# The first nine tiles of a fused attention and channel-mix kernel in another order, with more warm-up and filler products

## The chip, the cores and the metric

The kernel runs on one core of one Trainium2 chip. The time is the device time of one execution in microseconds; lower is better. The kernel before takes 1877.62 us (median of 3 runs, 1877.34 to 1879.11).

## The reference

Queries attend to keys that are pooled 4x4 and projected (the values are the same as the keys). The result goes through a channel mix with a shift by one token: two mixes of a token with the one before it, a squared ReLU layer of width 1024, and a sigmoid gate.

```python
# B, C = 4, 128; N = 12288 tokens, 768 pooled keys, d_ff = 1024
kv_pool = kv.reshape(B, H // 4, 4, W // 4, 4, C).mean(axis=(2, 4))
k = v = kv_pool.reshape(B, -1, C) @ w_sr
s = (q @ k.transpose(0, 2, 1)) / np.sqrt(C)
a = np.exp(s - s.max(-1, keepdims=True)); a /= a.sum(-1, keepdims=True) + 1e-09
x = a @ v
x_prev = np.concatenate([zeros, x[:, :-1, :]], axis=1)
xk = mu_k * x + (1.0 - mu_k) * x_prev
xr = mu_r * x + (1.0 - mu_r) * x_prev
kk = np.maximum(xk @ w_k, 0.0)
out = 1.0 / (1.0 + np.exp(-(xr @ w_r))) * (kk * kk @ w_v)
```

## The kernel before, in words

The tokens are cut into 97 tiles: two of 256 tokens at the start, then tiles of 512. All is kept with the channel on the partitions. Numbers are split into a high and a low half (`qh`, `ql`; `xkh`, `xkl`; `kh`, `kl`; `wkh`, `wkl`), and products are summed over the halves. A tile runs through named steps, each on one engine; `.4` behind a name is the tile:

- `qf` loads the queries (SP), `qh` casts them (ACT), `ql` is the rest (POOL).
- `S0` to `S3`: six score products for each 128 tokens (PE) into a `big` buffer of PSUM, of which there are three. `nm` takes the maximum (DVE), `ex` the exponential `pe` and its sum (ACT), `rc` the reciprocal (DVE: a tensor_scalar and a reciprocal), `f1` and `f2` make the high and low half of the weights `pp` (ACT and DVE), and `tt` transposes them by DMA (SP) into `pT`.
- `AV0` to `AV5`: 18 products `px` (PE). `xek`, `xer` (ACT), `xk`, `xr` (DVE) mix with the token before, for which POOL copies one column (`xck`, `xcr`); `xkh`, `xrh` cast (DVE), `xkl`, `xrl` subtract (POOL).
- `z`: three products for the gate, then `th`, `E` (ACT), `T1`, `E1`, `g` (DVE; the profile shows them as `th` and `E`).
- `ha`, `hb`: the products `ph` of the first layer, in four groups, into `big`. `r` is the ReLU `rr` (ACT), `k2` its square `kk` (DVE for groups 0, 1 and 3, ACT for 2), `kh` the cast (ACT for 0, 1, 3; DVE for 2), `kl` the rest (POOL for 0 to 2, DVE for 3).
- `va`, `vb`: the products `pv` of the second layer, into the one `v` buffer; `o` multiplies by the gate (DVE), `so` stores (SP). The next tile's `pv` can start when `o` has read the buffer.

Ahead of the tiles stand one-time steps: the pooled keys of the first batch (`L_a`, `L_b` load, `ad`, `bd` add on DVE, `pa`, `pb` project on PE, `ks`, `kh0_`, `kb0_`, `kl0_` and the like store the halves `ks`, `ksh`, `ksb`, `ksl`), the weights (`L_`, `we_`, `wl_`, `wi_`, `wt_`, `wc_`, `wx_`, `wy_`, `wg_`, `wh_`, `wd_` of `wk`, `wv`, `wr`), and scales (`am`, `ex`, `dg`, `xm`, `xt`, `sv`, `uz`, `cz`, `cv`). `warm` is a row of products of constants `pw` at the start. The keys of the next batch are loaded and summed during the tiles (`L_kv`, `br`, which writes `acc`).

The order is a table of numbers. Every step is put on one heap with its number; `give` takes the least and emits the step's instructions, and each engine keeps that order:

```python
def add(self, when, name, fn, of):
    heapq.heappush(self.heap, (when, next(self.count), fn, name, of))

def give(self):
    while self.heap:
        heapq.heappop(self.heap)[2]()
```

`ONCE` has the numbers of the one-time steps, `EARLY` those of the first nine tiles (one table each), `WHEN` those of all tiles in the middle (plus 19.3 times the tile), `LATE` those of the last ones. The numbers only order the steps; semaphores between engines make them wait for what they need. Nearly every instruction shows line 41 in the profile, that of the helper which emits it, so groups are told by tiles. `BUSY` may name groups of filler products, which write a `pw` tile in the `v` buffer:

```python
for i, n in enumerate(BUSY):
    @once(f"busy{i}")
    def _(n=n):
        if not busy:
            busy.append(take("v", name="pw", shape=[P, 2 * P]))
        for _ in range(n):
            pe.matmul(busy[0], lhsT=ones_b, rhs=ones.bitcast(BF16), start=True, stop=True)
```

Of the kernel before, what the change touches and what calls it, by code (L numbers as in the profile page):

```python
# [80 lines left out]
def tile_kernel(ctx, tc, qT, kv0, kvw, wmu, w_k, w_v, w_r, outT):  # L81
# [85 lines left out]
    busy = []  # L167
    for i, n in enumerate(BUSY):
        @once(f"busy{i}")
# [661 lines left out]
    for i, (b, t0, W) in enumerate(spans):  # L831
# [24 lines left out]
WARM = 48  # L856
BUSY = []
# [56 lines left out]
        "xer": 99.976, "xek": 101.1, "xk": 102.223, "xkh": 107.841, "ha1": 108.964, "xkl": 110.088,  # L914
# [8 lines left out]
    },  # L923
    {
# [14 lines left out]
    },  # L939
    {  # L940
# [7 lines left out]
        "xek": 169.203, "xk": 171.66, "xr": 172.151, "xkh": 175.59, "xkl": 176.082, "xrh": 181.144,  # L948
# [8 lines left out]
    },  # L957
    {
# [7 lines left out]
        "xek": 182.079, "xer": 182.287, "xr": 182.391, "xk": 182.495, "xkh": 182.599,  # L966
# [225 lines left out]
```

## Time and profile before

| | |
|---|---|
| median of 3 runs | 1877.62 us |
| the profiled execution | 1877.43 us, of which the span from first to last instruction 1875.7 us |
| PE, DVE, ACT, POOL busy, share of the span | 98%, 94%, 91%, 62% |
| granted TensorE clock | 1.000 |
| DMA | 232.16 MB, mean 124 GB/s |

The profile is of one execution. Times are in us from its first instruction. A group's row gives its count, its busy time, the mean length of one in ns, and the idle time ahead of it; a row in order of time gives start and length, and in brackets how long the engine had stood idle and what ended that. PE is the matrix engine TensorE, DVE VectorE, ACT ScalarE, POOL GpSimd, SP the engine that issues the DMAs. A DVE row counts as busy from its start to its end, whatever it does between.

### The profile page before, as it was taken

How to read it: one execution, taken by the hardware profiler on the slowest of the kernel's cores; microseconds unless marked ns; L12 is line 12 of the kernel's file. 1: busy time of each engine (PE TensorE's matmuls, PEld its weight loads, DVE VectorE, ACT ScalarE, POOL GpSimd, SP SyncE). 2: the span in 40 equal slices, each digit the busy share in tenths (PEclk: the TensorE clock that was granted, in tenths of full speed). 3: DMA queues.
4: the chain of work that ended last, by engine and by line, in shares of the span. 5: the costliest groups of instructions: out<-in, count | busy, mean ns of one | idle time of the engine just before them, and what ended most of it. 6: DMA issues, size and time to landing. Idle time of an engine off the chain costs nothing.

```text
span 1875.7 us, 27101 instructions
## 1 busy us (share of the span) xinstructions
PE 1843.9 (98%) x8978; PEld 923.3 (49%) x9124; DVE 1766.3 (94%) x2559; ACT 1703.8 (91%) x2448; POOL 1165.0 (62%) x800
## 2 busy tenths in 40 slices
PE   8999999999999999999999999999999999999999
PEld 4544445444444444444545454544444444444444
DVE  7999999999999999999998999999999898989998
ACT  6988899999999999999999999999999999999987
POOL 2554657575666666666656575756665656666555
PEclk9999999999999999999999999999999999999999
DMA  7756665555656666555656565655564655555552
GB/s 248 151 119 138 137 129 130 103 117 115 118 113 140 136 141 140 125 112 107 127 107 141 130 145 133 143 117 113 102 128 102 121 104 116 110 112 108 104 110 57
DMA packets 644236, 232.16 MB, mean 124 GB/s; under 512 B 612352, under 2 KB 613120, under 8 KB 644096
## 3 DMA queue, kind: packets, MB, share of 16 engines
q1 hardware_dynamic: 644096, 230.43, 58.5%
q8 instruction: 72, 1.18, 0.3%
q14 instruction: 68, 0.56, 0.1%
HBM read 52.63 MB, written 25.17 MB: 41 GB/s over the span
## 4 chain that ended last, share of the span: by engine, by line
PE 85%; DVE 9%; issue 1%; ACT 1%; POOL 0%; DVEq 0%; ACTq 0%
PE ph L41 24%; PE pv L41 22%; PE S L41 18%; PE px L41 17%; PE pz L41 3%; DVE pp L41 2%; DVE nm L41 2%; DVE kk L41 1%; DVE rc L41 0%; DVE kl L41 0%; DVE E L41 0%; DVE xk L41 0%; DVE xr L41 0%; DVE ph L41 0%; DVE o L41 0%
## 5 line engine op out<-in xcount | busy, mean ns | idle before, releaser
L41 POOL TENSOR_TENSOR kl<-kk,kh 128x1024 bf16<-128x1024 f32 (+1 forms) x291 | 683.3, 2349 | 59.4 <-DVE kk L41 17.6
L41 POOL TENSOR_TENSOR xrl<-xr,xrh 128x512 f16<-128x512 f32 (+1 forms) x97 | 113.7, 1172 | 514.1 <-DVE xrh L41 508.2
L41 DVE TENSOR_REDUCE nm<-S 128x1 f32<-128x768 f32 x384 | 364.2, 949 | 70.2 <-PE S L41 69.2
L41 DVE SCALAR_TENSOR_TENSOR pp<-pe,rc,pp 128x768 f16<-128x768 f32 x384 | 419.3, 1110 | 7.8 <-ACT pp L41 7.8
L41 PE MATMUL px<-pT,vT 128*128 128x512 f16 (+1 forms) x1746 | 420.6, 377 | 0.6 <-ACT E L41 0.5
L41 ACT ACTIVATE rr<-ph 128x1024 f32<-128x1024 f32 (+1 forms) x388 | 390.7, 1008 | 32.9 <-PE ph L41 31.1
L41 ACT ACTIVATE pe<-S,nm 128x768 f32<-128x768 f32 x384 | 344.2, 896 | 60.2 <-DVE nm L41 58.7
L41 ACT ACTIVATE pp<-pe,rc 128x768 f16<-128x768 f32 x384 | 339.8, 930 | 44.0 <-ACT pe L41 36.8
L41 ACT ACTIVATE kh<-rr 128x1024 f16<-128x1024 f32 (+1 forms) x291 | 304.5, 1047 | 0.9
L41 PE MATMUL ph<-xkh,wkl 128*128 128x512 f16 (+1 forms) x776 | 292.1, 377 | 4.4 <-DVE kl L41 1.7
L41 PE MATMUL pv<-kh,wvl 128*128 128x512 f16 (+1 forms) x776 | 292.0, 377 | 2.8 <-DVE o L41 2.8
L41 PE MATMUL ph<-xkh,wkh 128*128 128x512 f16 (+1 forms) x776 | 292.1, 377 | 0.0
L41 PE MATMUL pv<-kh,wvh 128*128 128x512 f16 (+1 forms) x776 | 292.0, 377 | 0.0
L41 PEld LDWEIGHTS <-vT 128*128 128x128 f16 x1746 | 170.6, 98 | 201.4 <-issue 1.3
L41 PE MATMUL S<-ksb,ql 128*128 128x256 bf16 (+1 forms) x762 | 249.9, 328 | 7.9 <-ACT pe L41 2.5
L41 PEld LDWEIGHTS <-wkh 128*128 128x128 f16 x1552 | 151.6, 98 | 172.3 <-issue 3.4
L41 DVE TENSOR_TENSOR kk<-ph,rr 128x1024 f32<-128x1024 f32 (+1 forms) x194 | 233.8, 1207 | 2.3 <-ACT rr L41 2.1
L41 PEld LDWEIGHTS <-wvh 128*128 128x128 f16 x1552 | 151.7, 98 | 170.5 <-issue 1.4
L41 PE MATMUL ph<-xkl,wkh 128*128 128x512 f16 (+1 forms) x776 | 229.2, 377 | 2.2
L41 PE MATMUL S<-ksl,qh 128*128 128x256 bf16 (+1 forms) x723 | 214.9, 323 | 0.4
L41 PE MATMUL pv<-kl,wvh 128*128 128x512 bf16 (+1 forms) x681 | 206.6, 377 | 0.4
L41 POOL TENSOR_TENSOR xkl<-xk,xkh 128x512 f16<-128x512 f32 (+1 forms) x97 | 145.8, 1503 | 76.2 <-DVE xkh L41 74.6
(126 smaller groups left out, 2484.5 us busy)
## 6 DMA issues: line engine op xcount, KB each, us to landing
qf<-qT SPq DMA_DIRECT2D x95, 256.0 KB, 3.4
outT<-o SPq DMA_DIRECT2D x95, 256.0 KB, 3.0
kvt<-kvw SPq DMA_DIRECT2D x36, 512.0 KB, 4.1
pT<-pp SPq DMA_TRANSPOSE x384, 3.8
kva<-kv SPq DMA_DIRECT2D x8, 512.0 KB, 9.0
kvb<-kv SPq DMA_DIRECT2D x4, 512.0 KB, 5.5
raw<-moe_w_v SPq DMA_DIRECT2D x2, 512.0 KB, 5.4
raw<-moe_w_k SPq DMA_DIRECT2D x2, 512.0 KB, 7.8
```

The costliest lines, as they stand in the source:

```text
L41: return self.tc.keep_in_program_order(op(*args, **kwargs))
```

## The change

The tables `ONCE` and `EARLY` get other numbers, `WARM` goes from 48 to 62, and `BUSY` gets two groups, of 10 and 14 products. `WHEN`, `LATE` and all functions stay. Each engine gets the same instructions as before and PE 38 more. The two filler groups stand among the score steps of the third tile: ten behind `S1` of the second tile, ahead of `S0.2`, and fourteen between `S3.2` and `S2.2`. From a place in tile 8 to 12 on (which one, depends on the engine) every engine's list is the old one; on PE it is the step `vb1` of tile 8.

```diff
-WARM = 48
-BUSY = []
+WARM = 62
+BUSY = [10, 14]
...
 ONCE = {
-    "L_wv1": -98.877, "we_wv1": -97.753, "warm": -96.63, "L_wv0": -95.506, "we_wv0": -94.383,
...
+    "warm": -98.95, "L_wv0": -97.9, "mix": -96.85, "we_wv0": -95.8, "wl_wv0": -94.75,
...
+    "wz_wr0": 40.713, "wh_wr0": 41.763, "cz": 42.813, "sv": 43.863, "busy0": 47.713,
+    "wd_wr0": 56.464, "busy1": 64.515, "cv": 91.117, "uz": 92.167, "wd_wv0": 99.518,
 }
```

Three places, as the engines get them. The first is on ACT, where the first batch's keys are stored (`pk` is their sum in PSUM, the 128x512 part and the 128x256 part; `qh` of the first two tiles). Before:

```order
L41 CAST qh_345<-qf_343 128x256
L41 CAST qh_354<-qf_352 128x256
L41 ACTIVATE ksb_91<-pk_186 128x512
L41 ACTIVATE ks_88<-pk_320 128x256
L41 ACTIVATE ksh_89<-pk_320 128x256
L41 ACTIVATE ksb_91<-pk_320 128x256
```

And now:

```order
L41 ACTIVATE ksb_91<-pk_227 128x512
L41 ACTIVATE ks_88<-pk_332 128x256
L41 CAST qh_365<-qf_363 128x256
L41 ACTIVATE ksh_89<-pk_332 128x256
L41 ACTIVATE ksb_91<-pk_332 128x256
L41 ACTIVATE wvh_80<-top_219 128x512
L41 CAST qh_376<-qf_374 128x256
```

Both `qh` casts stood ahead of these; now one stands among them and one behind. The last `ksb` also came behind DVE's `ksl` of the same `pk` in the old order and waited for it; in the new order `ksl` comes behind `ksb` and waits for that.

The second is on DVE, where tile 5 ends and the weights of tile 9 are made (`o` of tile 5, `pp` of tile 9, `E` and `th` of tile 5, `ph`/`kk` of tiles 6 and 7). Before:

```order
L41 TENSOR_SCALAR th_1754<-th_1754 128x512
L41 SCALAR_TENSOR_TENSOR E_1756<-th_1754,E_1756 128x512
L41 SCALAR_TENSOR_TENSOR pp_1994<-pe_1909,rc_1962,pp_1994 128x768
L41 TENSOR_TENSOR ph_1982<-ph_1982,rr_2033 128x1024
L41 TENSOR_TENSOR o_2038<-pv_1877,E_1756 128x512
L41 TENSOR_TENSOR kk_2048<-ph_1989,rr_2046 128x1024
```

And now:

```order
L41 TENSOR_SCALAR rc_2039<-sm_2010 128x2
L41 RECIPROCAL rc_2039<-rc_2039 128x2
L41 TENSOR_TENSOR o_2051<-pv_1906,E_1842 128x512
L41 CAST kh_2053<-kk_1964 128x1024
L41 SCALAR_TENSOR_TENSOR pp_2033<-pe_1970,rc_2013,pp_2033 128x768
L41 TENSOR_TENSOR kk_2095<-ph_2042,rr_2093 128x1024
```

`o` stood two rows behind the `pp` and now stands two rows ahead of it; `kh` of tile 6, which came further down, stands between.

The third is on POOL, around the subtraction `xrl` of tile 4 (`kl` rows are of tiles 2 and 3, `xkl` and `xrl` of tile 4, `ql` of tile 8). Before:

```order
L41 TENSOR_TENSOR kl_1298<-kk_1202,kh_1265 128x1024
L41 TENSOR_TENSOR xkl_1337<-xk_1331,xkh_1335 128x512
L41 TENSOR_TENSOR ql_1349<-qf_1243,qh_1292 128x512
L41 COPY xer_1352<-xer_1189 128x1
L41 TENSOR_TENSOR kl_1377<-kk_1354,kh_1375 128x1024
L41 TENSOR_TENSOR xrl_1381<-xr_1321,xrh_1379 128x512
L41 TENSOR_TENSOR kl_1421<-kk_1307,kh_1419 128x1024
```

And now:

```order
L41 TENSOR_TENSOR xkl_1377<-xk_1311,xkh_1322 128x512
L41 TENSOR_TENSOR kl_1381<-kk_1350,kh_1379 128x1024
L41 TENSOR_TENSOR xrl_1448<-xr_1315,xrh_1446 128x512
L41 TENSOR_TENSOR kl_1475<-kk_1291,kh_1368 128x1024
L41 COPY xek_1503<-xek_1195 128x1
L41 TENSOR_TENSOR ql_1535<-qf_1277,qh_1482 128x512
L41 TENSOR_TENSOR kl_1583<-kk_1416,kh_1480 128x1024
```

`xrl` stood right behind the `kl` of tile 3's group 0 (`kl_1377`) and now stands ahead of it (`kl_1583`), behind that of group 2.

More of the change, by code (lines that the diff above doesn't have):

```diff
@@ L909 @@
     {
[4 rows of a table removed]
-        "xer": 99.976, "xek": 101.1, "xk": 102.223, "xkh": 107.841, "ha1": 108.964, "xkl": 110.088,
[8 rows of a table removed]
-    },
-    {
[14 rows of a table removed]
-    },
-    {
[7 rows of a table removed]
-        "xek": 169.203, "xk": 171.66, "xr": 172.151, "xkh": 175.59, "xkl": 176.082, "xrh": 181.144,
[8 rows of a table removed]
-    },
-    {
[7 rows of a table removed]
-        "xek": 182.079, "xer": 182.287, "xr": 182.391, "xk": 182.495, "xkh": 182.599,
[8 rows of a table removed]
-    },
-    {
[8 rows of a table removed]
-        "xkl": 192.008, "ha2": 194.652, "xrh": 195.263, "xrl": 195.466, "ha1": 204.221,
[7 rows of a table removed]
-    },
-    {
[7 rows of a table removed]
-        "xek": 205.499, "xer": 206.544, "xk": 206.776, "xr": 206.834, "xkh": 207.414,
-        "xkl": 207.472, "xrh": 215.306, "xrl": 215.439, "ha0": 223.246, "hb0": 223.613,
[7 rows of a table removed]
-    },
-    {
[7 rows of a table removed]
-        "xer": 224.786, "xek": 225.006, "xk": 225.08, "xr": 226.033, "xkh": 227.06, "xkl": 227.133,
[8 rows of a table removed]
-    },
-    {
[7 rows of a table removed]
-        "xer": 234.648, "xek": 234.717, "xk": 234.787, "xr": 234.995, "xkh": 237.986, "xkl": 241.29,
[8 rows of a table removed]
-    },
-    {
[7 rows of a table removed]
-        "xer": 254.114, "xek": 254.889, "xk": 256.108, "xr": 259.322, "xrh": 259.437,
-        "xkh": 259.748, "xkl": 259.813, "xrl": 259.878, "ha1": 262.827, "hb1": 263.344,
[7 rows of a table removed]
[4 rows of a table added]
+        "xek": 84.817, "xer": 85.867, "xk": 86.917, "xr": 89.017, "xkh": 93.217, "xkl": 103.718,
[8 rows of a table added]
+    },
+    {
[4 rows of a table added]
+        "xck": 142.572, "xer": 146.772, "xr": 147.822, "xk": 148.872, "xkh": 163.717,
+        "xrh": 164.162, "xrl": 164.384, "ha2": 171.105, "ha1": 171.834, "xkl": 173.292,
[7 rows of a table added]
+    },
+    {
[7 rows of a table added]
+        "xer": 170.012, "xr": 170.741, "xrh": 172.563, "xkh": 172.928, "ha0": 178.778,
[8 rows of a table added]
+    },
+    {
[6 rows of a table added]
+        "AV5": 179.786, "AV2": 179.849, "xer": 180.038, "xek": 180.164, "xcr": 180.919,
+        "xr": 180.982, "xck": 181.045, "xk": 181.297, "xkh": 182.242, "xkl": 183.628, "xrh": 183.88,
[8 rows of a table added]
+    },
+    {
[7 rows of a table added]
+        "xek": 187.969, "xer": 190.252, "xk": 190.627, "xr": 191.001, "xkh": 191.564,
+        "xkl": 195.311, "xrh": 204.932, "xrl": 204.988, "ha2": 205.322, "ha1": 205.378,
[7 rows of a table added]
+    },
+    {
[7 rows of a table added]
+        "xek": 206.325, "xer": 206.437, "xck": 206.883, "xk": 206.938, "xr": 207.05, "xkh": 207.663,
[8 rows of a table added]
+    },
+    {
[7 rows of a table added]
+        "xer": 227.553, "xek": 227.559, "xk": 227.564, "xkh": 227.57, "xkl": 227.576, "xr": 227.648,
[8 rows of a table added]
+    },
+    {
[7 rows of a table added]
+        "xer": 233.895, "xek": 234.184, "xr": 234.91, "xk": 234.947, "xkh": 235.473, "xkl": 235.55,
[8 rows of a table added]
+    },
+    {
[8 rows of a table added]
+        "xrh": 259.293, "xrl": 259.466, "xkh": 264.05, "xkl": 265.428, "ha1": 265.516,
[7 rows of a table added]
     },
```

295 rows, old and new, of tables (EARLY, ONCE) are left out of this document.

## The prediction

> **What bounds the kernel now.** I read the page first, then the busy time by stretch, then the groups of DVE instructions in two stretches, then the instructions in order of time where PE stands still.
>
> ```profile
> core 0: us, PE busy (x) PEld busy (x) DVE busy (x) ACT busy (x) POOL busy (x), PEclk, DMA share, GB/s
> 27.00:48.00 21.00, 14.92 (x86) 9.19 (x86) 19.16 (x37) 19.17 (x38) 11.05 (x18) 1.00 0.72 143
> 48.00:221.00 173.00, 162.03 (x829) 83.96 (x843) 171.53 (x233) 152.51 (x228) 99.01 (x77) 1.00 0.63 134
> 221.00:410.00 189.00, 188.21 (x914) 93.88 (x928) 181.40 (x266) 172.52 (x249) 122.36 (x80) 1.00 0.56 121
> 410.00:600.00 190.00, 189.21 (x920) 94.08 (x934) 178.00 (x258) 176.96 (x253) 120.10 (x80) 1.00 0.61 122
> ```
>
> From 221 us on PE is busy all but 0.8 us in 190: TensorE bounds the steady part, which the change does not touch. In the nine tiles that it re-orders, PE idles 6.1 us (27 to 48) and 11.0 us (48 to 221), and DVE is the full engine: 171.53 of 173. So the time of the whole kernel moves by how much earlier or later PE gets to the first product behind which both orders hand out the same list (in tile 8, near 222 us), and up to there DVE sets the pace.
>
> DVE is full partly because its instructions are held. Here are the same forms in 48 to 221, and under them in ten steady tiles (599 to 788):
>
> ```profile
> L41 DVE SCALAR_TENSOR_TENSOR pp<-pe,rc,pp 128x768 f16<-128x768 f32 x36 | 40.7, 1147 | 0.0
> L41 DVE TENSOR_SCALAR rc<-sm 128x2 f32<-128x2 f32 x18 | 12.4, 690 | 0.1
> L41 DVE CAST xrh<-xr 128x512 f16<-128x512 f32 x8 | 6.2, 773 | 0.0
> L41 DVE SCALAR_TENSOR_TENSOR E<-th,E 128x512 f32<-128x512 f32 x7 | 5.8, 826 | 0.2
> L41 DVE TENSOR_SCALAR E<-E,sc 128x512 f32<-128x512 f32 x7 | 4.3, 617 | 0.0
> L41 DVE TENSOR_SCALAR th<-th 128x512 int32<-128x512 int32 x7 | 3.6, 521 | 0.0
> ...
> L41 DVE CAST xrh<-xr 128x512 f16<-128x512 f32 x10 | 4.2, 421 | 0.0
> L41 DVE TENSOR_SCALAR rc<-sm 128x2 f32<-128x2 f32 x20 | 3.2, 162 | 0.0
> L41 DVE SCALAR_TENSOR_TENSOR E<-th,E 128x512 f32<-128x512 f32 x10 | 6.9, 686 | 0.0
> L41 DVE TENSOR_SCALAR E<-E,sc 128x512 f32<-128x512 f32 x10 | 4.8, 479 | 0.0
> L41 DVE TENSOR_SCALAR th<-th 128x512 int32<-128x512 int32 x10 | 4.2, 422 | 0.0
> ```
>
> The excess is (690-162)x18 = 9.5 us for `rc`, (773-421)x8 = 2.8 for `xrh`, about 1.0 each for `E` (two forms), 0.7 for `th`, and (1147-1010)x36 = 4.9 for `pp`, whose bare time is the 1.01 of the 45.90 row below: 19.9 us in all. What holds them is seen in order of time (DVE, POOL, PE):
>
> ```profile
> 45.90 1.01 DVE L41 SCALAR_TENSOR_TENSOR pp<-pe,rc,pp 128x768 f16<-128x768 f32 x1
> 110.18 2.35 DVE L41 CAST xrh<-xr 128x512 f16<-128x512 f32 x1
> 110.11 2.13 POOL L41 TENSOR_TENSOR kl<-kk,kh 128x1024 bf16<-128x1024 f32 x1
> 173.53 2.89 DVE L41 SCALAR_TENSOR_TENSOR pp<-pe,rc,pp 128x768 f16<-128x768 f32 x1
> 176.34 1.22 DVE L41 TENSOR_TENSOR ph<-ph,rr 128x1024 f32<-128x1024 f32 x1
> 177.47 0.68 DVE L41 TENSOR_TENSOR o<-pv,E 128x512 f32<-128x512 f32 x1
> 173.33 2.27 POOL L41 TENSOR_TENSOR kl<-kk,kh 128x1024 bf16<-128x1024 f32 x1 [5.91 <-ACT kh L41]
> 174.46 1.46 PE L41 MATMUL px<-pT,vT 128*128 128x512 f16 x6
> 178.20 0.39 PE L41 MATMUL pv<-kh,wvl 128*128 128x512 f16 x1 [2.29 <-DVE o L41]
> ```
>
> The cast that takes 0.42 alone starts at 110.18 inside a POOL subtraction (110.11 to 112.24) and ends at 112.53; the `pp` at 173.53 is held until POOL's `kl` ends, `o` stands two rows behind it, and PE waits 2.29 us for `o`. So a DVE instruction that works in SBUF alone and starts inside a POOL subtraction lasts until that subtraction ends. 24 DVE rows of that kind end just behind a POOL row in the stretch (the `rc` at 58.39 is the first, the last a `g` at 218.69): 19.9/24 = 0.83 us a place.
>
> The Trainium skill (SBUF — State Buffer, "Who interferes with whom") calls this an exclusive lock on a shared port pair, which the first comer holds for its whole instruction. By that rule the later one may as well be POOL, so that some places would cost DVE nothing. That is the third rival below.
>
> **The change, part by part.** 14 more warm-up products: the 48 stand here.
>
> ```profile
> 1.18 8.11 PE L41 MATMUL pw<-ones,ones_b 128*128 128x256 bf16 x48 [1.18 <-DVE edge L106]
> 1.00:6.00 5.00, 4.82 (x23) 1.00 0.73 214
> 7.00:9.00 2.00, 2.00 (x20) 1.00 1.03 418
> 9.90 0.69 DVE L41 SCALAR_TENSOR_TENSOR top<-raw,ei 128x512 uint32<-128x512 uint32 x1 [1.25 <-ACT ei L41]
> ```
>
> The second and third rows count them in stretches: about 0.21 us each at first, 0.10 to 0.11 at the end. So 14 cost 14x0.109 = 1.5 us and end near 10.6, and the product that now follows them (`wc_wv0`) needs the `top` row that ends at 10.6. I cost them at 0; the DMA that fills the start covers them, and without it they would cost 1.5.
>
> The 24 fillers (10 and 14) take 24x0.109 = 2.6 us of PE, behind `S1.1` and behind `S3.2` of the third tile, ahead of the first tile's first `ha`. PE idles 6.1 us in that stretch, so I take 0; with that cover gone, 2.6. They write the `v` buffer, which nothing else holds until the first `pv`.
>
> The start: all loads are the same bytes in another order, and the last pooled load is still last.
>
> ```profile
> 24.37 0.69 DVE L41 TENSOR_TENSOR kvb<-kvb 128x512 f32<-128x512 f32 x1 [0.44 <-DMA kvb<-kv]
> 28.12 0.95 DVE L41 TENSOR_REDUCE ex<-ks 128x1 f32<-128x768 f32 x1 [1.11 <-ACT ks L41]
> 28.99 0.42 DVE L41 SCALAR_TENSOR_TENSOR ksl<-pk,ksh 128x256 bf16<-128x256 f32 x1
> 29.43 0.38 ACT L41 ACTIVATE ksb<-pk 128x256 bf16<-128x256 f32 x1 [1.08 <-DVE ksl L41]
> 30.29 0.96 DVE L41 TENSOR_REDUCE nm<-S 128x1 f32<-128x768 f32 x1 [0.25 <-PE S L41]
> 47.79 0.27 DVE L41 CAST xkh<-xk 128x256 f16<-128x256 f32 x1
> 210.33 0.69 DVE L41 TENSOR_TENSOR o<-pv,E 128x512 f32<-128x512 f32 x1
> ```
>
> DVE waits for a `kvb` load at 24.37, so the start goes at the pace of the loads, and the same loads in another order do not shorten it. What changes is behind it: `ksb` no longer waits 1.08 us for `ksl`, and `ks` is not queued behind a second `qh`. I place the first `nm` 0.4 us earlier, between 0 (it stays at the four `ex` steps on DVE) and 1.1 (the whole wait).
>
> The nine tiles: for a DVE step, PE reaches the common point no sooner than the DVE work up to that step plus the PE work behind the product that it releases. I added DVE's bare durations in both orders from the first `nm` (held instructions at their steady length, back to back), and PE's at 0.216 us for a 512-column product (the six `px` above: (1.46-0.38)/5) and 1.01 for a score step, from the chain:
>
> ```profile
> 610.71 2.02 PE S L41 x12
> ```
>
> Step; DVE ahead, before and after; PE behind, before and after; sums:
> - `xkh.0` (its row ends at 48.06, 17.8 after the first `nm`): 16.9, 16.4; 159.8, 159.8; 176.7, 176.2
> - `o.4`: 106.9, 109.8; 61.2, 61.2; 168.1, 171.0
> - `o.5`: 127.4, 124.4; 42.9, 45.3; 170.3, 169.7
> - `kh2.6`: 134.0, 125.0; 34.3, 45.3; 168.3, 170.3
> - `xkh.8`: 137.1, 140.5; 29.9, 28.6; 167.0, 169.1
> - `o.7`: 156.9, 155.3; 11.0, 10.1; 167.9, 165.4
>
> Before, `o.7` ended at 211.0 (its row), 180.7 after the first `nm`, so 23.8 us of holding and small gaps lay ahead of it; 180.7+11.0 = 191.7 decides (222.0 in the trace). By `xkh.0` alone it would be 176.7: the first 9 us of holding are free, every one beyond costs one. After the change, with holding at the same rate (23.8/156.9 = 0.152 per us of work), `xkh.8` decides: 169.1+0.152x140.5 = 190.5, a gain of 1.2. That part is the order alone. SP's queue gets the same transposes in nearly the same sequence, with `qf` loads and output issues put between at other places. What SP waits for is seen in its longest row:
>
> ```profile
> SPq L41 <- DVE pp L41: 1022.7, 262, 11.2
> ```
>
> It stands behind DVE's `pp`, so DVE's pace covers its moves; should an output that waits for `o` hold a transpose up, the next `px` products are late.
>
> How much is held is the large term. Laying POOL's list beside DVE's with those durations, I count 21 POOL instructions in the new order that have an SBUF-only DVE step right behind their release, against 23 in the old one. Some plain ones vanish (`xrl` of tile 4 now stands ahead of the `kl` that held the cast at 110.18; `o.5` stands ahead of the `pp` at 173.53), others appear (the `pp` step `f22.7` behind `kl0.4`, `f20.10` behind `kl0.7`). At 21/23 of the rate, `xkh.8` gives 169.1+0.139x140.5 = 188.6. From both sides: nothing held gives the 176.2 of `xkh.0`, a gain of 15.9; 31 places instead of 23 give 169.1+0.205x140.5 = 197.9, a loss of 6. I take 21, nearest to the rows.
>
> Sum: 0.4 (start) + 191.7-188.6 = 3.1 (tiles) = 3.5 us off the profiled execution's 1877.43 (its span 1875.7 and 1.7 around it; 0.2 under the median of the runs, 1877.62): 1873.9.
>
> **The rivals.** *Holding is halved.* For it: the steady order holds only `pp`, so such orders exist. Against: the count. 169.1+0.076x140.5 = 179.8: a gain of 12.3, 1865.
>
> *More is held, slower.* The place is the new pairs, `f22.7` behind `kl0.4` and `f20.10` behind `kl0.7`, each with most of a 2.13 us subtraction still to run, and every hold shifts the pairs behind it. It decides once over 22.6 us are held ahead of `xkh.8` (191.7-169.1); at 31 places, 5.8 us slower at most after the start's gain: 1883. For it: both are full-length. Against: in total the count is lower.
>
> *The lock goes the other way.* POOL, not DVE, waits at the new pairs, since its release comes late; then DVE runs near 18 places: 169.1+0.119x140.5 = 185.8, a gain of 6.3, 1871. For it: POOL rows that last longer than their kind, as the 2.27 `kl` above against 2.13. Against: most rows show DVE waiting.
>
> *Nothing to be measured.* The order's 1.2 us and a hold more or less: 1876.
>
> *PE slows down in the third tile.* PE stood idle 2.29 us at 178.20 and the products behind it follow at 0.22, so no idle of this trace slows it. The Trainium skill (TensorE: Matmul & The Clock Gate, "What's actually happening") puts the fall to half clock at an idle window of about 3.4 us. By that rule the fillers do nothing unless the new order leaves such an idle; I estimate from that page at most 3.4/2 = 1.7 us of PE work lost if it does. The 13 us by which `xkh.0` is off the deciding sum would hide it, so it moves no chance.
>
> **How the numbers follow.** About 0.2% (3.8 us, under 1873.9 or over 1881.4) is what I take a measurement to tell from no change. Halved holding 0.14; lock on POOL's side 0.14; the forecast case 0.40, half of it on either side of the bound (its own range 1870 to 1877, two or three places up or down); nothing 0.14; more held 0.18, of which 0.16 past the bound. Faster 0.48, within 0.36, slower 0.16. The range leaves out the far half of the halved case and of the slower one: 1866 to 1880.5.
>
> **What would show it.** The first `nm` starts at 29.9; DVE stays over 98% busy from 48 us on; `rc` averages 0.5 to 0.7 us there; the 48 to 221 stretch shows PE idle of 7 to 9 us in place of 11.0; fillers with nothing waiting behind them; `o` of tile 7 ends near 208. I am wrong if ACT or a transpose ends PE's waits in these tiles, if DVE is idle for more than 2 us there, or if the holds come out under 15 or over 27 us.

## The result, and the profile after

The changed kernel takes 1868.81 us (median of 4 runs, 1867.72 to 1868.91) against 1878.36 for the kernel before, run beside it: a ratio of 0.9948, with a 95% interval of 0.9930 to 0.9965. That is 9.5 us, where 3.5 had been forecast. The profiled execution took 1867.72, its span is 1865.9.

The busy time by stretch of the changed kernel, as shown of the kernel before (PE, PEld, DVE, ACT, POOL, each with its instructions):

```profile
27.00:48.00 21.00, 17.08 (x109) 11.32 (x109) 19.84 (x35) 19.31 (x38) 12.06 (x21) 1.00 0.77 132
48.00:221.00 173.00, 169.54 (x874) 89.07 (x889) 164.56 (x245) 159.83 (x240) 104.12 (x80) 1.00 0.68 142
221.00:410.00 189.00, 188.21 (x914) 93.82 (x928) 182.02 (x268) 174.22 (x250) 122.02 (x80) 1.00 0.57 122
```

PE idles 3.5 us in 48 to 221, in place of 11.0, and DVE, which was full (171.53 of 173), now stands still for 8.4 us. The steady part is as it was. The `o` of tile 10, in the middle of what both kernels hand out alike, stands so (before, then after):

```profile
259.88 0.68 DVE L41 TENSOR_TENSOR o<-pv,E 128x512 f32<-128x512 f32 x1
```

```profile
250.43 0.69 DVE L41 TENSOR_TENSOR o<-pv,E 128x512 f32<-128x512 f32 x1
```

So 9.4 us of the gain lie ahead of it. The groups of DVE instructions in 48 to 221, those of which the mean had been 1147, 690, 773, 826, 617 and 521 ns:

```profile
L41 DVE SCALAR_TENSOR_TENSOR pp<-pe,rc,pp 128x768 f16<-128x768 f32 x38 | 39.7, 1054 | 0.1
L41 DVE SCALAR_TENSOR_TENSOR E<-th,E 128x512 f32<-128x512 f32 x7 | 4.9, 693 | 0.1
L41 DVE TENSOR_SCALAR rc<-sm 128x2 f32<-128x2 f32 x18 | 3.8, 214 | 0.8 <-ACT pe L41 0.8
L41 DVE CAST xrh<-xr 128x512 f16<-128x512 f32 x8 | 3.5, 438 | 0.0
L41 DVE TENSOR_SCALAR E<-E,sc 128x512 f32<-128x512 f32 x7 | 3.3, 477 | 0.0
L41 DVE TENSOR_SCALAR th<-th 128x512 int32<-128x512 int32 x7 | 2.9, 417 | 0.0
```

By the prediction's own sum the holding is now (1054-1010)x38 = 1.7 us for `pp`, (214-162)x18 = 0.9 for `rc` and 0.1 for `xrh`: 2.7 us in place of 19.9. Nearly all of it is gone, where the forecast had 2 places of 23 go. How, the two pairs show that the prediction had named as new holds, `f22.7` with `kl0.4` and `f20.10` with `kl0.7`. In order of time (DVE's row of two ends with `f22.7` at 134.37, ACT's row of two ends with the `kh` that `kl0.7` reads at 187.12):

```profile
132.43 1.94 DVE L41 SCALAR_TENSOR_TENSOR pp<-pe,rc,pp 128x768 f16<-128x768 f32 x2
134.21 2.15 POOL L41 TENSOR_TENSOR kl<-kk,kh 128x1024 bf16<-128x1024 f32 x1 [3.85 <-ACT kh L41]
135.79 1.23 DVE L41 TENSOR_TENSOR kk<-ph,rr 128x1024 f32<-128x1024 f32 x1 [1.42 <-ACT rr L41]
185.12 2.00 ACT L41 ACTIVATE kh<-rr 128x1024 f16<-128x1024 f32 x2
186.20 1.01 DVE L41 SCALAR_TENSOR_TENSOR pp<-pe,rc,pp 128x768 f16<-128x768 f32 x1
187.20 2.14 POOL L41 TENSOR_TENSOR kl<-kk,kh 128x1024 bf16<-128x1024 f32 x1 [2.97 <-DMA qf<-qT]
188.28 1.23 DVE L41 TENSOR_TENSOR kk<-ph,rr 128x1024 f32<-128x1024 f32 x1 [1.07 <-ACT rr L41]
```

In both, `pp` is there first and lasts its bare 1.01; POOL's subtraction, released late by ACT's `kh`, begins as `pp` ends (0.16 us before its end in the first pair), and then lasts its bare 2.1 as well. The second bracket names a `qf` load, but the `kh` ended last, 0.08 us before the subtraction starts. Beside the subtraction DVE first waits for ACT's `rr` (1.42 and 1.07 us) and then runs a `kk`, which reads PSUM and lasts its usual 1.23. So at these two places neither engine is held.

The holding has not moved over to POOL either. Its largest group in 48 to 221, before and then after:

```profile
L41 POOL TENSOR_TENSOR kl<-kk,kh 128x1024 bf16<-128x1024 f32 x21 | 47.0, 2242 | 25.3 <-ACT kh L41 6.2 <-ACT xer L41 5.5 <-DVE kk L41 5.1
```

```profile
L41 POOL TENSOR_TENSOR kl<-kk,kh 128x1024 bf16<-128x1024 f32 x23 | 52.4, 2278 | 27.9 <-DVE kh L41 13.5 <-ACT kh L41 11.4 <-DMA qf<-qT 3.0
```

Some of POOL's rows are longer than their kind in both kernels. Over all its subtractions in this stretch, the time above the shortest of each kind is 10.0 us before and 9.1 after. What went are meetings in which POOL's row came first.

What still ends PE's waits, and the rows of ACT and DVE that go with the second:

```profile
48.39 0.27 PE L41 MATMUL ph<-xkh,wkl 128*128 128x256 f16 x1 [1.26 <-ACT pp L41]
69.46 0.27 PE L41 MATMUL ph<-xkh,wkl 128*128 128x256 f16 x1 [1.81 <-ACT pe L41]
67.02 0.69 ACT L41 ACTIVATE xer<-px,s 128x512 f32<-128x512 f32 x1 [1.70 <-DVE xk L41]
68.43 0.89 ACT L41 ACTIVATE pe<-S,nm 128x768 f32<-128x768 f32 x1
66.24 0.74 DVE L41 SCALAR_TENSOR_TENSOR xk<-px,s,xek 128x512 f32<-128x512 f32 x1
```

At 48.39 the named `pp` had long been done; it was `xkh.0`, which ended at 48.24. At 69.46 PE waits for a `big` buffer that `ex3.4` reads until 69.3; `ex3.4` stands on ACT behind `xer.2`, and `xer.2` waits until DVE's `xk.2` has read the same `px`.

The fillers:

```profile
33.25 1.26 PE L41 MATMUL pw<-ones,ones_b 128*128 128x256 bf16 x10
34.67 0.39 PE L41 MATMUL S<-ksb,ql 128*128 128x512 bf16 x1 [0.16 <-ACT pp L41]
38.56 1.69 PE L41 MATMUL pw<-ones,ones_b 128*128 128x256 bf16 x14
40.98 0.70 PE L41 MATMUL S<-ksb,ql 128*128 128x512 bf16 x2 [0.73 <-ACT pe L41]
```

Behind each group PE still waits for another engine (0.16 and 0.73), so they delay nothing.

### The profile page after: what moved, and what is told of

Read it like the earlier page. It is cut to its first block, busy times and chain, and to the rows that moved or that the text cites. A ratio compares the mean times of both kernels' runs of the same rounds, so it can differ in the third digit from the quotient of the medians.

```text
span 1865.9 us, 27185 instructions
## 1 busy us (share of the span) xinstructions
PE 1845.1 (99%) x9016; PEld 927.4 (50%) x9162; DVE 1752.1 (94%) x2559; ACT 1703.2 (91%) x2448; POOL 1162.8 (62%) x800
## 4 chain that ended last, share of the span: by engine, by line
PE 93%; DVE 4%; issue 1%; DMA 1%; ACT 1%; SPq 0%; POOL 0%; DVEq 0%; POOLq 0%; ACTq 0%
PE ph L41 26%; PE pv L41 24%; PE S L41 20%; PE px L41 19%; PE pz L41 4%; DVE pp L41 1%; DVE nm L41 1%; DMA kva<-kv 1%; DVE kk L41 0%; PE pk L41 0%; DMA raw<-moe_w_k 0%; DMA qf<-qT 0%; DVE o L41 0%; DVE xk L41 0%; DVE xr L41 0%
## 5 line engine op out<-in xcount | busy, mean ns | idle before, releaser
L41 PE MATMUL S<-ksb,ql 128*128 128x512 bf16 (+1 forms) x763 | 250.2, 328 | 4.4 <-ACT pe L41 1.8
L41 PE MATMUL S<-ksh,qh 128*128 128x512 f32 (+1 forms) x768 | 187.7, 362 | 1.5 <-ACT qh L41 0.8
```

The lines of the kernel that those rows point to most:

```text
L41: return self.tc.keep_in_program_order(op(*args, **kwargs))
```

## The experiments

For every run I took the held time row by row: each DVE row from 27 to 222 us less the usual length of its kind in that run. Beside it stands the length of the re-ordered part, from the start of the first `nm` to the end of `o.10`, which leaves out that the start comes up to 1.9 us later in some profiles. The latest is that of the last row, which is of the slowest of its five runs.

| kernel | held, us | first `nm` to `o.10`, us | median, us | ratio to before (95%) |
|---|---|---|---|---|
| before | 19.8 | 230.3 | 1878.4 | |
| before, 62 warm-up products | 20.0 | 231.4 | 1878.2 | 0.9998 (0.9988 to 1.0007) |
| before, three steps moved | 16.5 | 227.0 | 1875.6 | 0.9986 (0.9977 to 0.9995) |
| before, POOL copies | 11.7 | 222.1 | 1869.1 | 0.9950 (0.9938 to 0.9963) |
| changed | 4.7 | 221.3 | 1868.8 | 0.9948 (0.9930 to 0.9965) |
| changed, no fillers | 4.4 | 221.6 | 1868.3 | 0.9949 (0.9937 to 0.9962) |
| changed, no fillers, 48 warm-up | 4.7 | 221.9 | 1869.6 | 0.9953 (0.9940 to 0.9967) |
| changed, POOL copies | 11.3 | 226.5 | 1873.5 | 0.9972 (0.9962 to 0.9982) |
| changed, four pairs undone | 10.5 | 226.1 | 1872.6 | 0.9971 (0.9960 to 0.9981) |
| changed, `nm` of tiles 4, 5 twice | 4.9 | 228.2 | 1874.7 | 0.9982 (0.9974 to 0.9991) |
| changed, `nm` of tiles 7, 8 twice | 6.9 | 228.5 | 1876.0 | 0.9984 (0.9976 to 0.9993) |
| changed, four steps moved, `ex3.4` among them | 4.0 | 221.4 | 1867.7 | 0.9944 (0.9932 to 0.9957) |
| changed, three steps moved, `xer.2` among them | 3.4 | 219.3 | 1866.5 | 0.9940 (0.9927 to 0.9952) |

**Is it the holding? POOL copies in place of subtractions.**

```diff
             def _(f=f):
+                if kv[f] != "3" and i < len(EARLY):
+                    pool.tensor_copy(out=new(f"kl{f}"), in_=st[f"kk{f}"])
+                    return
                 (dve if kv[f] == "3" else pool).tensor_tensor(
```

In the kernel before:

> The kernel before, but POOL copies kk into kl in the first nine tiles in place of subtracting kh (the subtraction is left out there, so the second-layer products get another operand). Theory (POOL subtractions hold DVE, and the holds beyond the first 9 us cost one for one): 13 of the 24 held places stand at a kl; if a copy holds nothing, about 12 of the 19.8 us go, PE idle in 48 to 221 falls from 11.0 to 3 to 5 us, and the time is 1868 to 1871. Rival (the order of the steps, not the holding, is what cost): the holding may go, but PE waits at the same places; 1875 to 1878. Third (a copy holds DVE too, only for its own shorter time): holds of about half the length, 1871 to 1874.

In the changed kernel:

> The changed kernel with the same copies in place of the kl subtractions in the first nine tiles (the subtraction is left out there). Theory (holding is already nearly gone, 4.7 us, and PE sets the pace from 48 us on): no gain beyond 0.8 us, 1868.0 to 1869. Rival (DVE still paces these tiles): the remaining holds give 2 to 4 us, 1865 to 1867.

Measured: 1869.05 and 1873.53. The kernel before, with its order as it was, comes to within 0.3 us of the changed one: its holds fell by 8.1 us, where 12 had been expected, and its re-ordered part by 8.2. That speaks against the rival that the order as such had cost the time. The copies also shorten POOL's own work and make `kl` ready sooner, which this run doesn't separate from the holds; but in the kernel before no wait of a PE product in 48 to 221 is ended by a POOL row, and the runs with single steps moved, below, leave POOL's work as it is. The third theory is true as well, a copy on POOL does hold DVE:

```profile
48.00:221.00 173.00, 169.98 (x883) 88.33 (x884) 170.29 (x241) 158.60 (x237) 76.64 (x82) 1.00 0.67 141
106.46 1.04 POOL L41 CAST kl<-kk 128x1024 bf16<-128x1024 f32 x1
106.53 1.25 DVE L41 CAST xrh<-xr 128x512 f16<-128x512 f32 x1
```

The `xrh.4` that lasted 2.35 behind a subtraction lasts 1.25 behind a copy of 1.04.

The changed kernel became 4.7 us slower by the same edit, which neither theory had. POOL has less to do there, and its rows come to lie elsewhere:

```profile
150.29 1.33 POOL L41 TENSOR_TENSOR xrl<-xr,xrh 128x512 f16<-128x512 f32 x1 [3.09 <-DVE xrh L41]
150.64 1.53 DVE L41 SCALAR_TENSOR_TENSOR E<-th,E 128x512 f32<-128x512 f32 x1
151.57 1.50 POOL L41 CAST kl<-kk 128x1024 bf16<-128x1024 f32 x1
152.09 1.00 DVE L41 TENSOR_SCALAR rc<-sm 128x2 f32<-128x2 f32 x1
154.72 0.68 DVE L41 TENSOR_TENSOR o<-pv,E 128x512 f32<-128x512 f32 x1
155.46 0.39 PE L41 MATMUL pv<-kl,wvh 128*128 128x512 bf16 x1 [1.11 <-DVE o L41]
```

`g.4` (the `E<-th,E`) is held by `xrl.6`, `rc3.8` by the copy behind it, and PE waits for the `o.4` that follows. Held time rose from 4.7 to 11.3. So few holds are a matter of which row of POOL lies beside which of DVE, and not of how much POOL does.

**Single places.** Three steps of the kernel before, moved out of the way:

```diff
+EARLY[5]["f22"] = 190.8
+EARLY[4]["xrh"] = 191.5
+EARLY[5]["k23"] = 227.6
```

> The kernel before with three steps moved out of the way of a POOL subtraction: f22.5 behind nm3.6 (held 1.88 us by kl1.3), xrh.4 ahead of xkh.4 (held 1.93 by kl0.3), k23.5 behind rc3.8, so that rc3.8 starts ahead of kl0.5 (held 1.89). PE's, ACT's and POOL's own lists are unchanged. Theory A (holds are single places that can be taken out one by one): 5.7 us less held in 48 to 221, 14 in place of 19.8, and 1872.5 to 1874.5. Theory B (each place taken out shifts the later pairs, and others take their stead): held 17 to 23 us, and 1876 to 1880.

Measured: 1875.62, which is 2.7 us faster than the kernel before in the same series and lies between the two theories. 5.7 us of holds were taken out, and 3.3 are gone in the sum: one new hold is the `rc1.6` that now meets the same `kl1.3`:

```profile
100.42 2.85 POOL L41 TENSOR_TENSOR kl<-kk,kh 128x1024 bf16<-128x1024 f32 x1
102.07 1.23 DVE L41 TENSOR_SCALAR rc<-sm 128x2 f32<-128x2 f32 x1
```

What went was worth its length, 3.3 us of held time for 3.3 us of the re-ordered part (230.3 to 227.0).

And the other way, four steps of the changed kernel put beside a subtraction:

```diff
+EARLY[6]["f23"] = 206.74
+EARLY[5]["E1"] = 229.9
+EARLY[5]["T1"] = 234.0
+EARLY[8]["xrh"] = 256.95
```

> The changed kernel with four DVE steps moved by one or two places, so that each starts inside a POOL subtraction: f23.6 behind nm3.7 (into kl0.3), E1.5 behind k23.5 (into kl1.5), T1.5 ahead of xr.7 (into kl2.5), xrh.8 ahead of xk.8 (into kl0.6). PE's, ACT's and POOL's lists are unchanged. Theory A (the order of neighbours alone decides what is held; PE paces behind 70 us, so DVE has room there): held time in 48 to 221 rises by 1.4+1.4+1.4+1.7 = 5.9 us, to 9 to 11, but the places lie 10 to 30 us apart and DVE waits in between, so the time rises by 0 to 2 us, 1868.8 to 1870.8. Theory B (holds cost one for one here too): 1873.5 to 1875.5. Theory C (other pairs shift and give it back): held time under 8 us.

Measured: 1872.58, between the ranges of the first two theories. Held time rose by 5.8, as the first theory had it; but the time rose by 3.8 and the re-ordered part by 4.8, nearer to one for one. One of the places, with PE's wait behind it:

```profile
150.00 2.13 POOL L41 TENSOR_TENSOR kl<-kk,kh 128x1024 bf16<-128x1024 f32 x1 [5.28 <-ACT kh L41]
150.66 1.75 DVE L41 TENSOR_SCALAR E<-E,sc 128x512 f32<-128x512 f32 x1
153.07 1.04 PE L41 MATMUL pv<-kl,wvh 128*128 128x512 bf16 x3 [0.52 <-DVE o L41]
```

Four moves by one or two places, with no instruction added and no other engine's list touched, took back 3.8 of the 9.5 us.

**Does DVE have room behind PE after the change?** Eight more `nm`, in tiles 4 and 5 or, with `(7, 8)` in the first line, in tiles 7 and 8:

```diff
+                if i in (4, 5):
+                    dve.tensor_reduce(
+                        out=one("extra"), in_=st[f"S{s}"][:, :K], axis=AX.X, op=ALU.max, negate=True,
+                    )
```

> The changed kernel with eight nm more (tiles 4 and 5: each maximum is taken a second time, into a scratch column): 8x0.95 = 7.6 us more DVE work that no POOL row holds, all before 80 us. Theory A (DVE has some 8 us of slack behind PE after the change, and the holds stay where they are): 1868.8 to 1870.5, held time in 48 to 221 still 4 to 7 us. Theory B (few holds are a matter of how POOL's and DVE's rows happen to lie, as the copy on POOL showed, where they rose from 4.7 to 11.3 us): a shifted DVE meets POOL elsewhere, the holds rise to 10 us or more, and 1872 to 1877.

> The changed kernel with eight nm more, as in the run with the maxima of tiles 4 and 5 taken twice, but of tiles 7 and 8 (some 118 to 150 us), again 7.6 us more DVE work that nothing holds. There the time rose by 5.9 us. Theory A (DVE paces up to 70 us, and behind that it has some 8 us of room behind PE): 1868.8 to 1871, o.7 no more than 3 us later than 199.4. Theory B (DVE work costs nearly one for one anywhere in the nine tiles): 1873.5 to 1876.5.

Measured: 1874.70 and 1875.97, that is 5.9 and 7.2 us for 7.6 us of work. The theory that DVE's 8 us of idle time would take the work up falls both times. In the early run the second theory's mechanism falls too, since the holds stayed (4.9, and 6.9 in the late run). The longest wait of PE in the early run with the clock behind it, and one wait in the late run with the rows ahead of it:

```profile
72.82 0.37 PE L41 MATMUL ph<-xkh,wkl 128*128 128x256 f16 x1 [3.47 <-ACT pe L41]
72.50:73.00 0.50, 0.18 (x2) 0.62 1.01 401
73.00:73.50 0.50, 0.50 (x4) 0.50 1.00 410
```

```profile
135.04 0.95 DVE L41 TENSOR_REDUCE extra<-S 128x1 f32<-128x768 f32 x1
136.09 0.90 ACT L41 ACTIVATE pe<-S,nm 128x768 f32<-128x768 f32 x1 [1.97 <-DVE extra L41]
137.18 0.39 PE L41 MATMUL ph<-xkh,wkl 128*128 128x512 f16 x1 [2.72 <-DVE kl L41]
```

The wait at 69.46 grew from 1.81 to 3.47, since `ex3.4` and `xk.2` stand behind the added rows; in the late run PE waits 2.72 us for a `kl3`, which stands behind two of them.

Two things besides DVE's time go into these costs. In the early run PE's granted clock falls to half from 72.6 to 76.0 us, behind that wait; I estimate from these figures that this cost 3.4/2 = 1.7 us of PE work, and all 11 runs of this kernel show a granted clock under 1.000. The profile of the late run has 1.000. And an added `nm` reads the same scores as `ex`: at 136.09 `ex` starts just behind the added row, not behind its own `nm`, and in the late run five such waits of ACT make 6.2 us. So the runs show that eight more `nm` at these places find no room. That other work, which no step waits for, would find none either, they do not show.

**The fillers and the warm-up.** With neither, with the warm-up alone, and the longer warm-up in the kernel before:

```diff
-WARM = 62
-BUSY = [10, 14]
+WARM = 48
+BUSY = []
```

> The changed kernel with 48 warm-up products and no fillers; all else is kept. Theory (the gain comes from fewer held VectorE instructions, PE's own slack hides the fillers): 1868.8 us within 0.8; the stretch 27 to 48 us shows PE idle of 6 to 7 us in place of 3.9, since the 24x0.109 = 2.6 us of fillers turn into idle time, and the first ha of tile 0 starts at 48.4 as before. Rival (the fillers keep TensorE fast, and that is the gain): products behind 33 us last twice as long for some us, and the time is over 1871.

```diff
-BUSY = [10, 14]
+BUSY = []
```

> The changed kernel without the fillers, its 62 warm-up products kept. The kernel with neither lost clock: the granted clock was 0.72 and 0.50 in 12 to 16 us, and its first nm came at 30.86 in place of 29.78. Theory A (the 14 warm-up products keep the clock up in the changed start, the fillers do nothing): clock 1.00 throughout, first nm at 29.6 to 29.9, and 1867.7 to 1869.0 like the changed kernel; PE idle 6 to 7 us in 27 to 48. Theory B (the fillers also earn something): clock below 1.00 between 33 and 48, xkh.0 later than 48.24, and 0.8 us or more above the changed kernel.

```diff
-WARM = 48
+WARM = 62
```

> The kernel before with 62 warm-up products in place of 48; all else is kept. Theory A (in the old start PE's clock is 1.00 with 48, so 14 more only fill idle time): 1877.5 to 1879.2, like the kernel before. Theory B (the products behind them, each 0.109 us, hold up wc_wv0 and the start by up to 1.5 us): 1879 to 1880.5.

Measured: 1869.60, 1868.28 and 1878.21. PE's busy time and granted clock in the run with neither, and then in the one with the warm-up alone:

```profile
12.00:14.00 2.00, 1.65 (x8) 0.72 1.03 422
14.00:16.00 2.00, 2.00 (x3) 0.50 1.03 420
```

```profile
36.00:38.00 2.00, 1.42 (x6) 0.72 0.36 67
38.00:40.00 2.00, 2.00 (x8) 0.50 1.13 210
```

With neither, the clock falls to half from 12.9 to 16.3 us, and the first `nm` starts at 30.86 in place of 29.78. With the warm-up kept it does not fall there, and the first `nm` starts at 30.12. Whether that is worth some 1 us at the start is not shown: the runs' times, 1868.70 to 1870.83 against 1867.96 to 1869.54, overlap, and in the other profiles with 62 products and the changed start the first `nm` comes anywhere from 29.54 to 31.65. Without the fillers the clock falls later, from 36.9 to 40.3, and nothing comes of it: the time is that of the changed kernel. The fillers do keep the clock up, as the second theory had it, in a stretch where DVE and not PE sets the pace. In the kernel before, 62 warm-up products are worth nothing (0.9998).

The clock does have a part in the times of the kernel before. Of its 56 executions beside these experiments, 24 have a granted clock of 1.000, with a median of 1877.73, and 32 one of 0.998 or 0.999, with a median of 1879.25; the four of the changed kernel all have 1.000. With like against like the gain is 8.9 us in place of 9.5. Where the clock fell in those 32 is not known, as the one profile of them has 1.000; with 62 warm-up products the profile of the same order has it at half from 42.1 to 45.5 us. Whether the fall costs the 1.5 us, or a late start brings both, stays open.

**The two waits that are left.** First try:

```diff
+EARLY[4]["ex3"] = 169.8
+EARLY[0]["xkh"] = 88.0
+EARLY[2]["rc3"] = 93.5
+ONCE["wd_wv0"] = 104.0
```

> The changed kernel with four numbers moved: xkh.0 ahead of xr.0, rc3.2 behind it, wd_wv0 (POOL) behind xkl.0, ex3.4 ahead of xer.2. Theory (after the change PE sets the pace from 48 us on, and only its two waits there of 1.42 us at 46.85 and 1.97 us at 67.38 are left): both shrink, a gain of 2.0 to 3.3 us on 1868.8, so 1865.5 to 1866.8. Rival (DVE still sets the pace in these tiles): DVE's total of work and holding is the same but for the one hold of 0.98, the gain is 1.0 at most, 1867.8 to 1868.8.

Measured: 1867.70, just under the rival's range, and a re-ordered part as long as the changed kernel's (221.4 against 221.3): the rival. `xkh.0` came 1.0 us earlier, and two other steps were late next:

```profile
51.49 0.27 PE L41 MATMUL ph<-xkh,wkl 128*128 128x256 f16 x1 [1.42 <-ACT pe L41]
69.40 0.27 PE L41 MATMUL pz<-xrh,wrl 128*128 128x256 f16 x1 [0.81 <-DVE xr L41]
```

With `rc3.2` put back, ACT's `f12.2` and all behind it came 1 us later; with `ex3.4` ahead of it, `xer.2` and then `xr.2` did. Second try, in which `xer.2` only gets handed out ahead of `xk.2`, so that it no longer waits for it:

```diff
+EARLY[0]["xkh"] = 88.0
+EARLY[2]["xer"] = 169.5
+ONCE["wd_wv0"] = 104.0
```

> The changed kernel with three numbers moved: xkh.0 ahead of xr.0, wd_wv0 (POOL) behind xkl.0, xer.2 handed out ahead of xk.2, so that ACT does not wait for xk (1.7 us at 65.3) and ex3.4, behind it on ACT, comes earlier. rc3.2 and ex3.4 stay where they were. Theory (PE paces from 48 us on, its two waits are ended by xkh.0 and ex3.4): the first shrinks by about 1.0, the second by about 1.5, and 1866.3 to 1867.8. Rival (ACT and DVE are both full in 48 to 70, so another step of theirs is late next, as it was when ex3.4 itself was moved): PE idle in 48 to 70 stays within 0.7 us of 2.8, and 1868.0 to 1869.

Measured: 1866.45 (1866.33 to 1867.60), 2.4 us under the changed kernel, the best of all. The stretch 48 to 70 of the changed kernel and of this one:

```profile
48.00:70.00 22.00, 19.16 (x132) 13.38 (x135) 20.24 (x36) 19.94 (x39) 10.75 (x12) 1.00 1.01 189
```

```profile
48.00:70.00 22.00, 20.84 (x146) 14.21 (x144) 21.49 (x40) 22.00 (x43) 12.06 (x14) 1.00 1.07 205
```

PE's idle time falls from 2.8 to 1.2 us, ACT has no gap any more, and the wait at 69.46 is gone. The re-ordered part is 219.3 us long.

## Why the prediction was right, and where it was wrong

- **The direction and its cause.** Right: POOL's rows hold DVE's, the change takes holds away, and the time falls. The moved steps show the cause in both directions: three out of the way of a subtraction made the old order faster, four put beside one made the new order slower. Over the runs with held time of 4.7 to 20 us, a microsecond of it was worth 1.0 in the old order (3.3 for 3.3, 8.2 for 8.1) and about 0.8 in the new one (4.8 for 5.8, 5.2 for 6.6).
- **The size: the step "how much is held" failed.** I counted 21 places in the new order against 23 in the old and took the holding at 21/23 of its rate, some 19.5 us ahead of `xkh.8`. It was 2.7 us in the stretch, and three rows are held by more than 0.3 us where 19 were. The count asked of each POOL instruction only whether an SBUF-only DVE step stands behind its release in the lists. Which of the two starts first, and whether the two meet at all, it did not ask. For `f22.7` and `f20.10` DVE came first, with POOL's release late, as the third rival had it; but POOL did not wait either, and over the stretch its own held time did not rise (10.0 us before, 9.1 after). So the lock did not go the other way: the meetings in which POOL came first went away, and those in which DVE came first stayed about as they were. No case of the prediction had that. The measured time lies between the third rival (1871) and the one of halved holding (1865), and in holding the result goes beyond both.
- **The stated range.** 1868.8 lies inside 1866 to 1880.5, but by the width of that range, which was luck: the case held likeliest was 1870 to 1877, and the holding from which its sum was made, some 19.5 us, came out at 2.7.
- **What caps the gain.** The bound "nothing held" was 176.2 by `xkh.0`, 15.9 us off in the prediction. The held time fell by 15.1 us, and 9.0 came out in the re-ordered part, since DVE's gaps between 27 and 222 us rose from 3.3 to 9.8. I had named `xkh.8` as the deciding step; by its sum (29.78+140.5+28.6 and some 3 held) PE would reach the common point at 202, and it came there at 212.4. The sum of `xkh.0` comes nearer: it ended at 48.24, and 159.8 of PE work behind it make 208.0. Of the other 4.4 us, 3.2 are PE's idle time up to the common point, as the wait at 69.46. So the sums were lower bounds that took DVE's rows back to back, which they are no longer. The runs with more `nm` show the other side: 10 us of room, as `xkh.8`'s sum has it, are not there for work at these places.
- **The start.** 0.4 us by the first `nm` at 29.9; it is at 29.78, 0.5 earlier. The number fits, but it is one profile: the same start gave 29.54 to 30.40 in the profiles of five other runs and 31.65 in that of a sixth.
- **Warm-up and fillers at 0.** Right for the fillers, and for the warm-up in the old order. In the new one, in the one profile of each, the 14 products avert a fall of the clock at 12.9 us, which I had not seen, since the profile of the kernel before had 1.000 with 48; what that is worth is not shown. The 62 products end at 11.04 us; by the prediction's own rows (9.29 and 1.5) it is 10.8, and not the 10.6 that it gave.
- **The clock as a rival.** The fall happened without the fillers and was hidden, as the prediction said of it. The Trainium skill (TensorE: Matmul & The Clock Gate, "What's actually happening") ties it to an idle window of about 3.4 us. One fall fits that: in the run with `nm` of tiles 4 and 5 twice PE had stood idle for 3.47 us. The others don't need a window that is idle throughout: with neither warm-up nor fillers the clock fell at 12.9 us behind a stretch in which the single gaps of PE were 0.77, 0.72 and 0.35 us, and it did not fall in that same run at a gap of 2.26 us (39.8 to 42.1). Each fall lasted 3.4 us. What decides it stays open.
- **The signs.** Fillers with nothing behind them: right. DVE busy over 98%: it was 95 (164.56 of 173). `rc` at 0.5 to 0.7: 0.21. PE idle of 7 to 9: 3.5. `o.7` near 208: it ended at 199.4. Of the three things that would make it wrong, all came: ACT ends PE's longest wait, DVE is idle for 8.4 us, and the holds are under 15.

## What to carry to other kernels

Where DVE is full, look for its SBUF-only instructions (casts, a two-element `tensor_scalar`, products of two SBUF tensors) that end just as a row of POOL ends: each was worth 0.8 to 1.0 of its excess here, and moving a neighbour that reads PSUM between them costs no instruction. The lists of two engines don't tell which of a pair starts first, so a count of such pairs from the order is no size; only rows in time are, and any edit that shifts one engine against the other (less work on POOL too) deals the pairs anew. Once a wait is taken out, idle time summed over a stretch need not be room for more work: ask at the place where the work goes in, and what else waits for it.

## What the runs showed of the hardware that I had not expected

- A copy with a cast on POOL (1.04 us) holds DVE as a subtraction does; a 0.16 us `rc` lasted 1.00 behind one.
- Less work for POOL made the kernel 4.7 us slower (1873.53 against 1868.81), with 6.6 us more held time.
- Not every DVE instruction that works in SBUF alone is held, as the prediction had it: in the kernel before, a RECIPROCAL starts inside a POOL subtraction and lasts its usual 0.17 us.

```profile
132.39 2.13 POOL L41 TENSOR_TENSOR kl<-kk,kh 128x1024 bf16<-128x1024 f32 x1
132.49 0.17 DVE L41 RECIPROCAL rc<-rc 128x2 f32<-128x2 f32 x1
```

- PE's clock fell to half for 3.4 us at a time, once behind a gap of 3.47 us and once behind several short gaps of which none was over 0.8 us, and it stayed up at a gap of 2.26 us.
